# Attention, MLP, Fourier mixer and MLP on one core: steps of the query's tail, the mixers and the last pass in other slots, 32 adds on another engine

## The chip, the cores and the metric

The kernel runs on one core of a Trainium2 chip. What counts is the device time of one execution in microseconds, as the median of several runs. TensorE (PE in the profile) does the matmuls; VectorE (DVE), ScalarE (ACT) and GpSimd (POOL) work on tiles in SBUF, and the first two read the matmuls' results from PSUM banks; SyncE (SP) issues most of the DMAs in the order in which they are written.

## The reference

Three blocks stand one behind the other, each for 8 batches of 576 positions and 512 features:

```python
# 1. attention with 32 landmarks for each of 8 heads
A, Bm, C = sm(q, k_lm), sm(q_lm, k_lm), sm(q_lm, k)
Z = Bm.T / (norm1(Bm) * norminf(Bm) + 1e-6)
for _ in range(6):
    Z = 2 * Z - Z @ Bm @ Z
x = A @ Z @ C @ v
# 2. low-rank mix over positions, then an MLP of width 2048
u = x + (x.T @ U @ V).T
x = u + relu(u @ w_ch1) @ w_ch2
# 3. real part of a 2D Fourier transform, normalised, then a second MLP
u = x + real(fft(fft(x, axis=1), axis=2))
un = (u - mean(u)) / sqrt(var(u) + 1e-6)
out = u + relu(un @ w2_ch1) @ w2_ch2
```

The MLP weights come as 64-bit numbers.

## The kernel before

Every product of f32 matrices is made of three matmuls on high and low parts (`split`: ACT copies the high part, another engine subtracts it to get the low one). The 4608 positions are cut into 9 chunks of 512 columns, and an MLP pass (`Mlp.stream`) runs over the chunks with half of the hidden width: for each hidden block `up` does 12 matmuls (lines 299 to 301), ACT the relu (303) and DVE its low part (304); 4 output blocks follow (348 to 350) and DVE adds the residual (358). There are two such passes for the first MLP and one for the second; the second MLP's other half is done by `quarters`, a scheme with 7 products for two chunks in place of 8, in 10 units: chunk 0 alone, then four pairs, for p = 0 and again for p = 1. Each unit has slots of 6 matmuls, 16 in a unit of one chunk and 30 in one of two; `prepare` makes the next unit's high and low parts, `load` fetches chunks, and `down` adds the outputs: `get_res` loads an earlier partial result, `plant` has ACT copy it into a PSUM bank (538), `mul` adds three matmuls a block to it (547 to 549).

Everything is ordered by hand: nothing is moved by a scheduler. A stream gives way after each hidden or output block, that is after 12 matmuls: this is a slot. `Slots` is a table of (slot, step), and at each slot the steps of other work that are due are issued behind the stream's matmuls, on whichever engines they use. Every engine runs its own instructions in the order in which they were issued.

- The attention's `Batch.steps` (one batch every 16 slots, beside the first pass) has, at the end of each batch: normalising the query's scores A (`query_norm`, line 885 on DVE) at slot 12, transposing them (`query_t`, 891 and ACT's copies 893), their last 64 rows (`query_tail`, 900 and ACT's copies 903) at slot 14, and their products with U (`mixed`, 914) at slot 15. `query_tail` and `mixed` both use the bank "b", of which there is one. The Newton steps (932, 937) run beside them.
- `Mixer.steps` (one batch every 24 slots, from slot 33 of the second pass on) loads a batch of the first MLP's result (`load`, tile U), folds it by symmetry over features and positions (`fold_d` 1066, `fold_t` 1076), splits that (`fold_split`, tiles h and l with e or o for the even and odd part), makes a special row (`fold_row`), and multiplies by cosine and sine tables (`over_d`, matmuls 76 to 78, the row's at 1107). It ends with `unfold`, `store`, and the normalisation of two halves: `mean` (1160) sums over features with a matmul and DVE reads it (1170). `mean` uses the bank "l", of which there is one; the products use "f", of which there are two.
- `convert`, `single` and `stage` take weights from 64-bit integers to high and low f32 parts in five steps on DVE, ACT and POOL and put them to DRAM for the pass to come; `bufs` is the number of their buffers. Between them DVE waits for POOL's add (104 or 135).

On SP the loads for a chunk, the stores (213 to 216, 226), weight fetches (255, 88), the staged weights (119) and U's load (1057) stand in one queue, and a store waits at its head until its data is there.

Of the kernel before, what the change touches and what calls it, by code (L numbers as in the profile page):

```python
# [39 lines left out]
def body(ctx: ExitStack, tc: tile.TileContext, qT, kT, vn, mU, mV, w11, w12, w21, w22,  # L40
# [49 lines left out]
    def convert(cv, raw, out, bufs=1):  # L90
# [12 lines left out]
        nc.vector.scalar_tensor_tensor(out=pf, in0=lo, scalar=2.0 ** -52, in1=pf, op0=ALU.mult, op1=ALU.mult)  # L103
        nc.gpsimd.tensor_tensor(pf, pf, af, op=ALU.add)  # L104
        yield 1
# [15 lines left out]
    def single(cv, raw, out, bufs):  # L121
# [12 lines left out]
        nc.vector.scalar_tensor_tensor(out=pf, in0=lo, scalar=2.0 ** -52, in1=pf, op0=ALU.mult, op1=ALU.mult)  # L134
        nc.gpsimd.tensor_tensor(pf, pf, af, op=ALU.add)
        yield 1
# [99 lines left out]
    class Mlp:  # L236
# [154 lines left out]
        def quarters(self, tail, ys, w1s, w2s, dst):  # L391
# [89 lines left out]
            def up_two(i, s0, g):  # L481
# [23 lines left out]
                for q in range(2):  # L505
# [9 lines left out]
                    rectify(g, (0, 2 + q), B("e", q), s0 + 12 + q)  # L515

            def down(i, s0, g):
                p, unit = units[i]
                seed = i > 0
                res, skip, sc, ps, out = {}, {}, {}, {}, {}  # L520
                outs = [(h, d) for h in reversed(range(len(unit))) for d in range(4)]

                def get_res(j, c, d):
                    res[j] = lp.tile([P, NC], F32, name="res", bufs=4)
                    ys[p].get(c, d, res[j])

# [40 lines left out]
                for j, (h, d) in enumerate(outs):  # L567
                    c, s = unit[h], s0 + 2 * j
                    lag = 0 if end and j + 1 == len(outs) else 1
                    at(max(s - 10, s0 - 8 + j), lambda j=j, c=c, d=d: get_res(j, c, d))  # L570
                    at(s - 4, lambda j=j: plant(j))
# [23 lines left out]
            for i, (p, unit) in enumerate(units):  # L595
# [3 lines left out]
                def begin(i=i, s0=s0, g=g, two=two, last=last):  # L599
                    (up_two if two else up_one)(i, s0, g)  # L600
                    down(i, s0 + (14 if two else 8), g)
                    if i + 1 < len(units):
                        prepare(i + 1, s0, (2, 4, 13, 16, 19, 22, 25) if two else range(2, 16, 2) if i else range(7, 21, 2))
                    if i + 2 < len(units):
                        for key, s in (((0, 0), 10), ((1, 0), 24), ((1, 1), 27), ((0, 1), 29)):
                            if not two:
                                s = {10: 8, 24: 14, 27: 17, 29: 19}[s] + (5 if i == 0 else 0)
                            if key[0] < len(units[i + 2][1]):
                                at(s0 + s, lambda key=key: load(i + 2, key))
                    if last:  # L610
                        for n in range(7):
                            at(s0 + 2 * n + 3, lambda n=n: (self.w1.append(0), self.w1.pop(), self.fetch("w1", w1s[n])))
                        for d in range(4):
                            at(s0 + 24 + 2 * d, lambda d=d: self.fetch("w2", w2s[d]))
# [60 lines left out]
    class Batch:  # L675
# [308 lines left out]
        def steps(self, after):  # L984
# [8 lines left out]
            if not a:  # L993
# [6 lines left out]
                        (11, lambda: self.query_norm(H0)), (12, self.values), (12, lambda: self.query_norm(H1)),  # L1000
                        (13, lambda: self.query_t(0)), (14, lambda: self.query_t(1)), (14, self.query_tail),
                        (15, self.mixed), (16 - b, self.heads), (17 - b, self.rank))
# [41 lines left out]
    class Mixer:  # L1044
# [33 lines left out]
        def fold_split(self, nm):  # L1078
            h = self.fp.tile([P, 2, NF], F32R, name=f"h{nm}", bufs=1)
            l = self.fp.tile([P, 2, NF], F32R, name=f"l{nm}", bufs=1)  # L1080
            split(h, l, self.c[nm][:, :, 0:NF])
            self.lhs[nm] = (h, l)

        def fold_row(self):
            fp, U = self.fp, self.U
            row = fp.tile([1, NF], F32, name="top", bufs=1)
            nc.vector.tensor_tensor(row[:, 1:HS], U[0:1, 2, 1:HS], U[0:1, 2, S - 1:HS:-1], op=ALU.add)
            nc.scalar.copy(row[:, 0:NF:HS], U[0:1, 2, 0:NF:HS])
            both = self.f["row"]
            nc.scalar.copy(both[0:1], row)  # L1090
            low = fp.tile([1, NF], F32, name="rl", bufs=1)
            nc.vector.tensor_tensor(low, row, f32(both[0:1]), op=ALU.subtract)
            nc.scalar.copy(both[32:33], low)
# [64 lines left out]
        def mean(self, n):  # L1158
            ps = self.bank("l", 1)[:, 0:HS]
            nc.tensor.matmul(ps, self.f["ones"], self.half[n]["a"][:, 0, :], start=True, stop=True)  # L1160
            return ps
# [38 lines left out]
        def steps(self):  # L1200
            yield from ((0, self.load), (4, lambda: self.fold_d("e")), (4, lambda: self.fold_d("o")),
                        (5, lambda: self.fold_t("e")), (6, lambda: self.fold_split("e")), (6, self.fold_row),
                        (7, lambda: self.fold_t("o")), (8, lambda: self.fold_split("o")))
            yield from ((8 + 3 * (nm == "o") + i, lambda nm=nm, i=i: self.over_d(nm, i)) for nm in "eo"
                        for i in range(3))
            yield from ((14, self.top_row), (15, lambda: self.odd(0)), (16, lambda: self.even(0)),
# [245 lines left out]
```

## Time and profile before

| | |
|---|---|
| median of 3 runs | 1869.18 us (1866.18 to 1873.06) |
| profiled execution, its own time | 1866.1 us |
| its span in the trace | 1864.1 us |
| TensorE busy | 1824.5 us, 98% |
| DVE, ACT, POOL busy | 1024.1, 708.3, 376.2 us |

The span is the time from the first to the last instruction of the trace, 2.0 us less than the execution's own time. In the trace the attention ends at about 470 us, the mixers lie between 686 and 1322, and the quarters begin at 1485. A row of a timeline has the start, the length, the engine, the line of the kernel, the operation and its tiles (out<-in); in brackets stands how long the engine idled before it, and for whom. Instructions that belong together are drawn as one row with a count.

### The profile page before, as it was taken

The numbers are of one execution on the slowest core, as the hardware profiler recorded it, in microseconds if no ns is written. First come the engines' busy times: TensorE is split into PE (matmuls) and PEld (weight loads), VectorE is DVE, ScalarE is ACT, GpSimd is POOL, SyncE is SP. The second block draws the span as 40 slices with busy tenths as digits, with TensorE's granted clock in tenths as the row PEclk, the third lists the DMA queues.
The fourth block names the chain that finished last, engine by engine and source line by source line (L and its number), as shares of the span: only waits on it lengthen the run. The fifth ranks groups of instructions, "written<-read, shape, count | busy, mean of one in ns | idle before, by whom it ended". The sixth has DMA issues, their size and how long they took to land.

```text
span 1864.1 us, 30739 instructions
## 1 busy us (share of the span) xinstructions
PE 1824.5 (98%) x12152; PEld 1482.5 (80%) x12152; DVE 1024.1 (55%) x1764; ACT 708.3 (38%) x1469; POOL 376.2 (20%) x355
## 2 busy tenths in 40 slices
PE   6899999999999999999999999999999999999999
PEld 5777777777888887887887888888888888887887
DVE  7897565555323334755555464475432275438774
ACT  3544443444312212323333243333322266545542
POOL 3334211221201222323122142332311000000000
PEclk9999999999999999999999999999999999999999
DMA  7455445452537343434535553442432564477765
GB/s 266 140 179 162 148 168 201 143 172 98 172 124 276 125 135 113 153 111 168 170 128 190 220 176 137 142 150 79 167 111 88 183 193 157 144 259 226 225 198 158
DMA packets 175391, 305.56 MB, mean 164 GB/s; under 512 B 27440, under 2 KB 92560, under 8 KB 175248
## 3 DMA queue, kind: packets, MB, share of 16 engines
q1 hardware_dynamic: 170640, 294.17, 47.6%
q10 hardware_dynamic: 4608, 9.44, 1.3%
q8 instruction: 95, 1.56, 0.4%
q14 instruction: 48, 0.39, 0.1%
HBM read 195.74 MB, written 107.22 MB: 163 GB/s over the span
## 4 chain that ended last, share of the span: by engine, by line
PE 87%; DVE 5%; DMA 3%; ACT 3%; issue 1%; SPq 0%; POOL 0%; ACTq 0%; DVEq 0%
PE ps L348 10%; PE ps L349 10%; PE ps L350 10%; PE ps L299 9%; PE ps L301 9%; PE ps L300 9%; PE ps L549 3%; PE ps L547 3%; PE ps L548 3%; PE ps L387 3%; PE ps L389 3%; PE ps L388 3%; PE ps_f L76 1%; PE ps_f L77 1%; DMA U<-x 1%; PE ps_f L78 1%
## 5 line engine op out<-in xcount | busy, mean ns | idle before, releaser
L348 PE MATMUL ps<-g,w 128*128 128x512 f32 x864 | 345.5, 400 | 0.0
L299 PE MATMUL ps<-x,w 128*128 128x512 f32 x864 | 345.4, 400 | 0.0
L350 PE MATMUL ps<-g,w 128*128 128x512 f32 x864 | 338.5, 392 | 0.6 <-DVE g L304 0.6
L349 PE MATMUL ps<-g,w 128*128 128x512 f32 x864 | 338.1, 391 | 0.0
L301 PE MATMUL ps<-x,w 128*128 128x512 f32 x864 | 337.3, 390 | 0.0
L300 PE MATMUL ps<-x,w 128*128 128x512 f32 x864 | 337.0, 390 | 0.0
L304 DVE SCALAR_TENSOR_TENSOR g<-ps,g 128x512 fp32r<-128x512 f32 x216 | 148.7, 689 | 334.6 <-ACT g L303 333.9
L303 ACT ACTIVATE g<-ps 128x512 fp32r<-128x512 f32 x216 | 129.0, 597 | 368.2 <-PE ps L301 367.8
L348 PEld LDWEIGHTS ps<-g,w 128*128 128x128 f32 x864 | 162.9, 189 | 37.6 <-issue 3.5
L350 PEld LDWEIGHTS ps<-g,w 128*128 128x128 f32 x864 | 163.0, 189 | 36.3 <-DVE g L304 1.0
L301 PEld LDWEIGHTS ps<-x,w 128*128 128x128 f32 x864 | 162.2, 188 | 35.0
L299 PEld LDWEIGHTS ps<-x,w 128*128 128x128 f32 x864 | 162.2, 188 | 34.4
L349 PEld LDWEIGHTS ps<-g,w 128*128 128x128 f32 x864 | 163.2, 189 | 32.2
L300 PEld LDWEIGHTS ps<-x,w 128*128 128x128 f32 x864 | 162.5, 188 | 31.5
L104 POOL TENSOR_TENSOR cvp<-cvp,cva 128x512 f32<-128x512 f32 x56 | 72.8, 1300 | 380.8 <-DVE cvp L103 380.8
L358 DVE TENSOR_TENSOR xf<-ps,xf 128x512 f32<-128x512 f32 x76 | 52.4, 689 | 120.3 <-PE ps L350 116.8
L549 PE MATMUL ps<-g,w 128*128 128x512 f32 x288 | 112.3, 390 | 2.0 <-DVE g L457 2.0
L547 PE MATMUL ps<-g,w 128*128 128x512 f32 x288 | 112.3, 390 | 1.1 <-ACT ps L538 1.0
L52 POOL TENSOR_TENSOR x<-xf,x 128x512 fp32r<-128x512 f32 (+7 forms) x56 | 67.8, 1213 | 220.8 <-ACT x L51 193.8
L548 PE MATMUL ps<-g,w 128*128 128x512 f32 x288 | 112.0, 389 | 0.0
L52 POOL TENSOR_TENSOR stg<-cva,stg 128x512 fp32r<-128x512 f32 x40 | 57.3, 1433 | 68.4 <-ACT stg L51 66.7
L101 ACT ACTIVATE wraw<-wraw 128x512 f32<-128x512 f32 x48 | 32.7, 681 | 91.2 <-DVE cva L97 88.1
(325 smaller groups left out, 2915.9 us busy)
## 6 DMA issues: line engine op xcount, KB each, us to landing
d<-stg SPq DMA_DIRECT2D x54, 512.0 KB
w<-d SPq DMA_DIRECT2D x54, 512.0 KB
wraw<-w SPq DMA_DIRECT2D x48, 512.0 KB
y<-xf SPq DMA_DIRECT2D x76, 256.0 KB
res<-y SPq DMA_DIRECT2D x72, 256.0 KB
xf<-y SPq DMA_DIRECT2D x40, 256.0 KB
u<-u1T ACTq DMA_DIRECT2D x32, 288.0 KB
U<-x SPq DMA_DIRECT2D x8, 1152.0 KB
```

What stands on the lines that cost most here:

```text
L52: (eng or nc.vector).tensor_tensor(lo, src, f32(hi), op=ALU.subtract)
L299: nc.tensor.matmul(ps, wh, xh, start=k == 0, stop=False)
L300: nc.tensor.matmul(ps, wl, xh, start=False, stop=False)
L301: nc.tensor.matmul(ps, wh, xl, start=False, stop=k == 3)
L303: nc.scalar.activation(g[:, 0, :], ps, AF.Relu)
L304: nc.vector.scalar_tensor_tensor(out=g[:, 1, :], in0=ps, scalar=0.0, in1=f32(g[:, 0, :]), op0=ALU.max, op1=ALU.subtract)
L348: nc.tensor.matmul(ps, wh, gh, start=k == m0, stop=False)
L349: nc.tensor.matmul(ps, wl, gh, start=False, stop=False)
L350: nc.tensor.matmul(ps, wh, gl, start=False, stop=k == m1 - 1)
L547: nc.tensor.matmul(ps[j], wh, gh, start=first, stop=False, skip_group_check=True)
L548: nc.tensor.matmul(ps[j], wl, gh, start=False, stop=False, skip_group_check=True)
L549: nc.tensor.matmul(ps[j], wh, gl, start=False, stop=k == ks[3], skip_group_check=True)
```

## The change

It has four parts. In the attention `query_tail` is issued at slot 13 in place of 14. In the mixers U's load goes a slot earlier than the mixer's first (not for batch 0), the folds and the splits of their parts go a slot later and their high and low parts are steps of their own, the products follow from slot 9 instead of 8, and `mean` takes its bank from "f". In the conversions with one buffer the add goes from POOL to DVE. In the quarters, `res` of a unit of one chunk is loaded at the end of the unit before, and `prepare` and `load` have other slots at the unit bounds. The lines of the changed kernel are numbered 15 higher behind `quarters` and 23 higher behind `fold_row`.

```diff
@@ -101,7 +101,7 @@
         nc.scalar.activation(f32(hi), f32(hi), AF.Abs)
         pf, af = f32(p), f32(a)
         nc.vector.scalar_tensor_tensor(out=pf, in0=lo, scalar=2.0 ** -52, in1=pf, op0=ALU.mult, op1=ALU.mult)
-        nc.gpsimd.tensor_tensor(pf, pf, af, op=ALU.add)
+        (nc.gpsimd if bufs > 1 else nc.vector).tensor_tensor(pf, pf, af, op=ALU.add)
         yield 1
         nc.vector.scalar_tensor_tensor(out=af, in0=f32(hi), scalar=MINNORM, in1=pf, op0=ALU.is_ge, op1=ALU.mult)
         yield 1
@@ -132,7 +132,7 @@
         nc.scalar.activation(f32(hi), f32(hi), AF.Abs)
         pf, af = f32(p), f32(a)
         nc.vector.scalar_tensor_tensor(out=pf, in0=lo, scalar=2.0 ** -52, in1=pf, op0=ALU.mult, op1=ALU.mult)
-        nc.gpsimd.tensor_tensor(pf, pf, af, op=ALU.add)
+        nc.vector.tensor_tensor(pf, pf, af, op=ALU.add)
         yield 1
         nc.vector.scalar_tensor_tensor(out=out, in0=f32(hi), scalar=MINNORM, in1=pf, op0=ALU.is_ge, op1=ALU.mult)
         yield 1
@@ -514,15 +514,22 @@
                         rectify(g, key, T, s)
                     rectify(g, (0, 2 + q), B("e", q), s0 + 12 + q)
 
+            former = {}
+
+            def order(unit):
+                return [(h, d) for h in reversed(range(len(unit))) for d in range(4)]
+
+            def get_res(i, j):
+                p, unit = units[i]
+                h, d = order(unit)[j]
+                t = former.setdefault(i, {})[j] = lp.tile([P, NC], F32, name="res", bufs=4)
+                ys[p].get(unit[h], d, t)
+
             def down(i, s0, g):
                 p, unit = units[i]
                 seed = i > 0
-                res, skip, sc, ps, out = {}, {}, {}, {}, {}
-                outs = [(h, d) for h in reversed(range(len(unit))) for d in range(4)]
-
-                def get_res(j, c, d):
-                    res[j] = lp.tile([P, NC], F32, name="res", bufs=4)
-                    ys[p].get(c, d, res[j])
+                skip, sc, ps, out = {}, {}, {}, {}
+                outs, res = order(unit), former.setdefault(i, {})
 
                 def get_skip(j, c, d):
                     skip[j] = lp.tile([P, NC], F32, name="skip", bufs=4)
@@ -567,7 +574,8 @@
                 for j, (h, d) in enumerate(outs):
                     c, s = unit[h], s0 + 2 * j
                     lag = 0 if end and j + 1 == len(outs) else 1
-                    at(max(s - 10, s0 - 8 + j), lambda j=j, c=c, d=d: get_res(j, c, d))
+                    if len(unit) == 2 or i == 0:
+                        at(max(s - 10, s0 - 8 + j), lambda j=j: get_res(i, j))
                     at(s - 4, lambda j=j: plant(j))
                     for half in range(2):
                         at(s + half, lambda j=j, h=h, d=d, half=half: mul(j, h, d, half))
@@ -598,13 +606,20 @@
 
                 def begin(i=i, s0=s0, g=g, two=two, last=last):
                     (up_two if two else up_one)(i, s0, g)
+                    if i + 1 < len(units) and len(units[i + 1][1]) == 1:
+                        for j in range(4):
+                            at(s0 + 25 + j, lambda j=j: get_res(i + 1, j))
                     down(i, s0 + (14 if two else 8), g)
                     if i + 1 < len(units):
-                        prepare(i + 1, s0, (2, 4, 13, 16, 19, 22, 25) if two else range(2, 16, 2) if i else range(7, 21, 2))
+                        if two:
+                            starts = (2, 4, 13, 16, 19, 22, 25) if len(units[i - 1][1]) == 2 else (5, 13, 15, 17, 19, 22, 25)
+                        else:
+                            starts = (2, 4, 9, 11, 13, 15, 17) if i else range(8, 22, 2)
+                        prepare(i + 1, s0, starts)
                     if i + 2 < len(units):
                         for key, s in (((0, 0), 10), ((1, 0), 24), ((1, 1), 27), ((0, 1), 29)):
                             if not two:
-                                s = {10: 8, 24: 14, 27: 17, 29: 19}[s] + (5 if i == 0 else 0)
+                                s = {10: 8, 24: 18, 27: 20, 29: 22}[s] + (5 if i == 0 else 0)
                             if key[0] < len(units[i + 2][1]):
                                 at(s0 + s, lambda key=key: load(i + 2, key))
                     if last:
@@ -998,7 +1013,7 @@
                         (9, lambda: self.query_exp(H0)), (9, self.scores_sum), (10, lambda: self.scores_t(0)), (10, lambda: self.query(2)),
                         (11, lambda: self.scores_t(1)), (11, self.scores_tail), (11, lambda: self.query_exp(H1)),
                         (11, lambda: self.query_norm(H0)), (12, self.values), (12, lambda: self.query_norm(H1)),
-                        (13, lambda: self.query_t(0)), (14, lambda: self.query_t(1)), (14, self.query_tail),
+                        (13, lambda: self.query_t(0)), (13, self.query_tail), (14, lambda: self.query_t(1)),
                         (15, self.mixed), (16 - b, self.heads), (17 - b, self.rank))
             if self.b:
                 yield 13, lambda: self.mlp.get_tail(self.b)
@@ -1078,18 +1093,26 @@
         def fold_split(self, nm):
             h = self.fp.tile([P, 2, NF], F32R, name=f"h{nm}", bufs=1)
             l = self.fp.tile([P, 2, NF], F32R, name=f"l{nm}", bufs=1)
-            split(h, l, self.c[nm][:, :, 0:NF])
+            nc.scalar.copy(h, self.c[nm][:, :, 0:NF])
             self.lhs[nm] = (h, l)
 
+        def fold_low(self, nm):
+            h, l = self.lhs[nm]
+            nc.vector.tensor_tensor(l, self.c[nm][:, :, 0:NF], f32(h), op=ALU.subtract)
+
         def fold_row(self):
-            fp, U = self.fp, self.U
-            row = fp.tile([1, NF], F32, name="top", bufs=1)
+            U = self.U
+            self.row = row = self.fp.tile([1, NF], F32, name="top", bufs=1)
             nc.vector.tensor_tensor(row[:, 1:HS], U[0:1, 2, 1:HS], U[0:1, 2, S - 1:HS:-1], op=ALU.add)
             nc.scalar.copy(row[:, 0:NF:HS], U[0:1, 2, 0:NF:HS])
+
+        def row_high(self):
+            nc.scalar.copy(self.f["row"][0:1], self.row)
+
+        def row_low(self):
             both = self.f["row"]
-            nc.scalar.copy(both[0:1], row)
-            low = fp.tile([1, NF], F32, name="rl", bufs=1)
-            nc.vector.tensor_tensor(low, row, f32(both[0:1]), op=ALU.subtract)
+            low = self.fp.tile([1, NF], F32, name="rl", bufs=1)
+            nc.vector.tensor_tensor(low, self.row, f32(both[0:1]), op=ALU.subtract)
             nc.scalar.copy(both[32:33], low)
 
         def over_d(self, nm, i):
@@ -1156,7 +1179,7 @@
             nc.vector.tensor_tensor(a[:, 0, :], a[:, 0, :], a[:, 1, :], op=ALU.add)
 
         def mean(self, n):
-            ps = self.bank("l", 1)[:, 0:HS]
+            ps = self.bank("l")[:, 0:HS]
             nc.tensor.matmul(ps, self.f["ones"], self.half[n]["a"][:, 0, :], start=True, stop=True)
             return ps
 
@@ -1198,11 +1221,12 @@
             nc.sync.dma_start(rs[self.b][:, self.cols(n)], self.half[n]["r"])
 
         def steps(self):
-            yield from ((0, self.load), (4, lambda: self.fold_d("e")), (4, lambda: self.fold_d("o")),
-                        (5, lambda: self.fold_t("e")), (6, lambda: self.fold_split("e")), (6, self.fold_row),
-                        (7, lambda: self.fold_t("o")), (8, lambda: self.fold_split("o")))
-            yield from ((8 + 3 * (nm == "o") + i, lambda nm=nm, i=i: self.over_d(nm, i)) for nm in "eo"
-                        for i in range(3))
+            yield from ((-1 if self.b else 0, self.load), (5, lambda: self.fold_d("e")), (5, lambda: self.fold_d("o")),
+                        (6, lambda: self.fold_t("e")), (6, self.fold_row), (7, lambda: self.fold_split("e")),
+                        (7, self.row_high), (8, lambda: self.fold_low("e")), (8, self.row_low),
+                        (7, lambda: self.fold_t("o")), (8, lambda: self.fold_split("o")), (9, lambda: self.fold_low("o")))
+            yield from ((s, lambda nm=nm, i=i: self.over_d(nm, i)) for s, nm, i in
+                        ((9, "e", 0), (10, "e", 1), (11, "e", 2), (12, "o", 0), (13, "o", 1), (13, "o", 2)))
             yield from ((14, self.top_row), (15, lambda: self.odd(0)), (16, lambda: self.even(0)),
                         (17, lambda: self.unfold(0)), (17, lambda: self.unfold(2)), (17, lambda: self.odd(1)),
                         (18, lambda: self.even(1)), (19, lambda: self.unfold(1)), (19, lambda: self.unfold(3)),
```

On TensorE, in a batch of the attention: x and w belong to the MLP's stream, ps_n to a Newton step, ps_c to `query_t`, ps_b to `query_tail`. Before:

```order
L301 MATMUL ps<-x,w_256 128x512
L932 MATMUL ps_n<-ry 32x64 x8
L891 MATMUL ps_c<-ident_sb,A 128x128 x4
L299 MATMUL ps<-x,w_257 128x512
L300 MATMUL ps<-x,w_257 128x512
...
L301 MATMUL ps<-x,w_257 128x512
L932 MATMUL ps_n<-ry 32x32 x8
L891 MATMUL ps_c<-ident_sb,A 128x128 x4
L900 MATMUL ps_b<-ident_sb,A 64x64 x4
L348 MATMUL ps<-g,w_258 128x512
```

And of the changed kernel:

```order
L301 MATMUL ps<-x,w_256 128x512
L947 MATMUL ps_n<-ry 32x64 x8
L906 MATMUL ps_c<-ident_sb,A 128x128 x4
L915 MATMUL ps_b<-ident_sb,A 64x64 x4
L299 MATMUL ps<-x,w_257 128x512
...
L300 MATMUL ps<-x,w_257 128x512
L301 MATMUL ps<-x,w_257 128x512
L947 MATMUL ps_n<-ry 32x32 x8
L906 MATMUL ps_c<-ident_sb,A 128x128 x4
L348 MATMUL ps<-g,w_258 128x512
```

The tail's four matmuls moved from behind the second transposition to behind the first, ahead of a block of 12 matmuls of the stream.

On DVE, at the fold of mixer 0: L304 is the MLP's, L358 its residual add, x and xf its next chunk, wraw, cva and cvp a weight that is converted, big and cc the folds, le, lo and rl the low parts. Before:

```order
L304 SCALAR_TENSOR_TENSOR g<-ps,g 128x512
L1066 TENSOR_TENSOR big<-U 128x1152
L106 SCALAR_TENSOR_TENSOR cva<-wraw,cvp 128x512
L304 SCALAR_TENSOR_TENSOR g<-ps,g 128x512
L1076 TENSOR_TENSOR cc<-big 128x2x287
L304 SCALAR_TENSOR_TENSOR g<-ps,g 128x512
L52 TENSOR_TENSOR le<-cc,he 128x578
L1087 TENSOR_TENSOR top<-U 1x287
L1092 TENSOR_TENSOR rl<-top,row 1x289
L52 TENSOR_TENSOR x<-xf,x 128x512
L358 TENSOR_TENSOR xf<-ps,xf 128x512
L52 TENSOR_TENSOR lo<-cc,ho 128x578
```

And of the changed kernel:

```order
L104 TENSOR_TENSOR cvp<-cvp,cva 128x512
L304 SCALAR_TENSOR_TENSOR g<-ps,g 128x512
L106 SCALAR_TENSOR_TENSOR cva<-wraw,cvp 128x512
L304 SCALAR_TENSOR_TENSOR g<-ps,g 128x512
L1081 TENSOR_TENSOR big<-U 128x1152
L304 SCALAR_TENSOR_TENSOR g<-ps,g 128x512
L1091 TENSOR_TENSOR cc<-big 128x2x287
L1106 TENSOR_TENSOR top<-U 1x287
L52 TENSOR_TENSOR x<-xf,x 128x512
L358 TENSOR_TENSOR xf<-ps,xf 128x512
L1101 TENSOR_TENSOR le<-cc,he 128x578
L1115 TENSOR_TENSOR rl<-top,row 1x289
```

The fold of U stands one L304 lower, the low parts `le` and `rl` stand behind the split of x and the residual add instead of ahead of them, and the conversion's add (L104) has come onto this queue.

On SP, around the end of mixer 1 and the load of U for mixer 2: x_3 and x_4 are results of the first MLP, u_1 the mixed batch, d_9 a staged weight, un_184 its normalised half. Before:

```order
L1146 DMA u_1_176<-U 128x4x576
...
L216 DMA x_4_74<-xf 1x256
L119 DMA d_9_146<-stg 128x1024
L88 DMA wraw<-w 128x1024
L223 DMA xf<-y_5_83 128x512 x4
L1195 DMA un_184<-Z 128x4x288
L1057 DMA U<-x_2_72 128x4x576
L1195 DMA un_184<-Z 128x4x288
```

And of the changed kernel:

```order
L1169 DMA u_1_176<-U 128x4x576
...
L216 DMA x_4_74<-xf 1x256
L1072 DMA U<-x_2_72 128x4x576
L119 DMA d_9_146<-stg 128x1024
L88 DMA wraw<-w 128x1024
L223 DMA xf<-y_5_83 128x512 x4
L1218 DMA un_184<-Z 128x4x288 x2
```

The load of U moved from between the stores of the two halves to right behind the last store of x_4, ahead of the staging's two DMAs and the stream's loads.

## Rows read from the trace of the kernel before

**Rows 1.** The page, part 1: busy time, share and count by engine.

```profile
PE 1824.5 (98%) x12152; PEld 1482.5 (80%) x12152; DVE 1024.1 (55%) x1764; ACT 708.3 (38%) x1469; POOL 376.2 (20%) x355
```

**Rows 2.** Waits of PE: releaser; total us, times, longest.

```profile
PE ps_b L914 <- ACT at L903: 4.1, 7, 1.8
PE ps_f L1107 <- ACT row L1093: 3.0, 3, 1.0
...
PE ps_l L1160 <- DVE Z L1170: 2.2, 2, 1.1
PE ps L549 <- DVE g L457: 2.0, 2, 1.7
...
PE ps_f L77 <- DVE le L52: 1.4, 3, 0.5
PE ps L547 <- ACT ps L538: 1.0, 1, 1.0
PE ps L350 <- DVE g L304: 0.6, 1, 0.6
```

**Rows 3.** PE timeline, mixer 0: start, us, line, [idle before <-releaser].

```profile
698.55 0.40 PE L348 MATMUL ps<-g,w 128*128 128x512 f32 x1
698.78 0.40 PE L349 MATMUL ps<-g,w 128*128 128x512 f32 x1
699.74 0.49 PE L350 MATMUL ps<-g,w 128*128 128x512 f32 x1 [0.56 <-DVE g L304]
...
702.72 0.43 PE L1107 MATMUL ps_f<-tabh,row 128*97 128x258 f32 x1 [0.99 <-ACT row L1093]
```

**Rows 4.** Windows: length, busy us (instructions) by engine, PEclk, DMA share, GB/s.

```profile
86.00:96.00 10.00, 8.11 (x136) 6.42 (x132) 8.96 (x15) 6.45 (x18) 7.00 (x10) 0.83 0.01 2
696.00:706.00 10.00, 7.91 (x30) 5.74 (x30) 6.80 (x9) 4.51 (x10) 6.72 (x6) 0.84 0.34 114
1676.00:1690.00 14.00, 10.88 (x44) 7.83 (x44) 9.19 (x15) 7.87 (x15) 0.00 (x0) 1.00 0.80 279
```

**Rows 5.** Timeline of batch 1.

```profile
80.78 0.48 PE L299 MATMUL ps<-x,w 128*128 128x512 f32 x1
...
81.62 0.82 DVE L885 TENSOR_TENSOR A<-A,sr 128x640 f32<-128x640 f32 x1
...
85.60 0.43 PE L932 MATMUL ps_n<-ry 32*32 32x64 f32 x16 [1.80 <-DVE ry L937]
```

**Rows 6.** Timeline of batch 2.

```profile
139.56 0.82 DVE L885 TENSOR_TENSOR A<-A,sr 128x640 f32<-128x640 f32 x1
...
139.72 0.48 PE L299 MATMUL ps<-x,w 128*128 128x512 f32 x1
```

**Rows 7.** Timeline of batch 5.

```profile
322.03 0.82 DVE L885 TENSOR_TENSOR A<-A,sr 128x640 f32<-128x640 f32 x1
...
322.56 0.48 PE L299 MATMUL ps<-x,w 128*128 128x512 f32 x1
```

**Rows 8.** DVE and POOL in the timeline, mixer 0.

```profile
693.97 1.36 DVE L1066 TENSOR_TENSOR big<-U 128x1152 f32<-128x1152 f32 x1 [2.48 <-DMA U<-x]
...
694.01 2.60 POOL L1066 TENSOR_TENSOR big<-U 128x576 f32<-128x576 f32 x1 [1.82 <-DMA U<-x]
...
695.25 1.92 DVE L106 SCALAR_TENSOR_TENSOR cva<-wraw,cvp 128x512 f32<-128x512 f32 x1
```

**Rows 9.** SP's timeline, around the load of U for mixer 2.

```profile
835.56 5.43 SPq L216 DMA_DIRECT2D x<-xf  x1
...
846.89 0.44 SPq L1057 DMA_DIRECT2D U<-x  x1
```

**Rows 10.** The page, part 5: busy us, mean ns.

```profile
L104 POOL TENSOR_TENSOR cvp<-cvp,cva 128x512 f32<-128x512 f32 x56 | 72.8, 1300 | 380.8 <-DVE cvp L103 380.8
...
L358 DVE TENSOR_TENSOR xf<-ps,xf 128x512 f32<-128x512 f32 x76 | 52.4, 689 | 120.3 <-PE ps L350 116.8
```

**Rows 11.** ACT timeline, quarters, unit 5.

```profile
1681.53 0.59 ACT L538 COPY ps<-res 128x512 f32<-128x512 f32 x1 [4.63 <-DMA res<-y]
```

## The prediction

> **What bounds the kernel now.** I read the busy shares first: TensorE is busy in 1824.5 of 1864.1 us, 98%, and no other engine is above 55% but its own weight loads [rows 1]. So the time is the matmuls plus what TensorE idles, 39.6 us, and a change that leaves the matmuls alone can win only there or in the clock. Next the waits of TensorE, by what it waited for [rows 2]. The diff touches seven of these rows: L914, L1107, L1160, L549, L77, L547 and L350, 4.1 + 3.0 + 2.2 + 2.0 + 1.4 + 1.0 + 0.6 = 14.3 us in 7 + 3 + 2 + 2 + 3 + 1 + 1 = 19 waits. Such a row understates the loss: two matmuls in a row start 0.23 us apart though each is drawn 0.40 us long [rows 3], so an idle of x costs x + 0.17. With 19 × 0.17 = 3.2 the 19 waits cost 17.5 us. By stage: attention (L914) 4.1 + 7 × 0.17 = 5.3; mixers 7.2 + 9 × 0.17 = 8.7; quarters 3.0 + 3 × 0.17 = 3.5.
>
> Last I looked at the granted clock in windows around those places [rows 4]. After the waits of batch 1 it averages 0.83 over 10 us, after those of mixer 0 0.84, so 10 × 0.17 = 1.7 and 10 × 0.16 = 1.6 us are lost to a spell at 1.2 in place of 2.4 GHz. In the quarters 14 us with 3 us of idle stay at 1.00. So a wait does not always cost clock, and I treat the clock as a term apart.
>
> **The change, part by part. Tail of the query.** `mixed` (L914) waits for ACT's copies (L903) of the one bank "b" that `query_tail` has just filled; with the tail a slot sooner those four copies have a slot more, 12 matmuls × 0.23 = 2.8 us, and the longest of the seven waits was 1.8. All seven should go: −5.3. The tail's four small matmuls now stand where the first `L299` stood, and they need A as normalised by DVE's L885. TensorE stops for that, with everything behind it on its queue, if L885 is late. Batch 1: L885 ends at 82.44, TensorE is there at 80.78, 1.66 late, but 5 us on TensorE waits 1.80 for a Newton step that DVE sets [rows 5], so this is idle moved, not added. Batch 2: 140.38 against 139.72, 0.66 late [rows 6]. Batch 5: 322.85 against 322.56, 0.29 late [rows 7]. In batches 3, 4, 6 and 7 the same pair of rows has L885 done first, and batch 0 idles there at start-up anyhow. Together +1.0; bounds 0 and 1.66 + 6 × 0.66 = 5.6.
>
> **Mixers.** DVE's fold of mixer 0 waits 2.48 us for U and holds the MLP's `L304` that is behind it [rows 8]; that is the wait of L350. U's load goes a slot or more earlier, ahead of the staging DMAs on SP: for mixer 2 SP comes free of the waiting L216 at 841.0 and issues U only at 846.89 [rows 9], now right behind it, some 5 us sooner. What SP is moved past are one staging write, one weight fetch and four loads for the stream, put off by one issue of 0.44 us. The fold itself begins a slot later (4 to 5). Mixer 0: without the wait it could begin at 693.97 − 2.48 + 2.76 = 694.25, 0.28 later than now, while its first product (slot 8 to 9) comes 2.76 later. Of this gain of 2.48, an x split and a residual add that now stand ahead of `le` on DVE take 2 × 0.69 = 1.4 (the price of such an operation is in [rows 10]), which leaves about 1.1 against the 0.5 that L77 waited at most; `rl` stands right behind `le` on DVE, and the row's copies on ACT then have the three products of a slot less to wait for. I take the waits of L77, L350 and L1107 as gone. The mean moves from one bank to two, so that a matmul no longer waits for DVE to read the other half's mean (L1160). Together −8.7. The margins are under 1 us, and DVE's rows before are no guide to mixers 1, 3, 5 and 7, which showed no such wait. I take eight new waits of 0.1, +0.8; bounds 0 and 8 × 0.99 = 7.9, the longest that a mixer shows [rows 3].
>
> **Adds from POOL to DVE.** In the conversions with one buffer 24 adds at L104 and 8 at L135 move. On POOL one takes 1300 ns, and a DVE operation of two inputs on the same tile 689 [rows 10]: POOL −41.6 us, DVE +22 us, 55% to 57% of the span. All lie from the mixers on, where DVE is busy 6.80 of 10 us [rows 4]; the staged weights are used a pass later, so nothing but DVE's queue carries the cost to TensorE. What hides it is DVE's 3.2 us in 10. If the cover is gone at an add, its 0.69 lies in front of an L304 that a matmul waits for. Taken at 0; bounds −0.6 and +22, the former because DVE's L106 no longer waits there for POOL, so that an L304 behind it could save a wait like that of L350.
>
> **Quarters.** Unit 5 is the first with p = 1. Its first `res` came to ACT 4.63 us late [rows 11], behind it stood the relu, and the three waits of TensorE in [rows 2] at L547 and L549 are this place. The loads move to the end of unit 4, 5 to 6 slots of 6 × 0.23 = 1.4 us sooner, 7 us where 4.63 were missing. −3.5. The preparation at the other unit bounds is spread out, and a few loads come up to 4 slots later; in unit 0 one is issued in the slot of its first use. One new wait of the size of L547's, +1.0; bounds 0 and 3.5.
>
> **Clock.** The spell after mixer 0 goes with all three waits before it: −1.6. That of batch 1 has lost one of its two waits; half of it, −0.85. Together −2.4; bounds 0 and −3.3.
>
> The Trainium skill, *SBUF — State Buffer*, section *SBUF: two separate sides*, speaks against the moved adds: DVE and GpSimd share one port pair as an exclusive lock, and a DVE operation with two SBUF inputs is held for the whole of a GpSimd operation that reads SBUF. The trace agrees where they met: the L106 at 695.25 took 1.92 us [rows 8] with the fold on POOL beside it from 694.01 on, against 0.69 for a two-input operation by itself [rows 10]. By this rule an add that meets such a fold costs the 1.92; were it so for all 32, the time would be that of rival 4.
>
> **The sum**, against the profiled execution's own 1866.1: −17.5 − 2.4 + 1.0 + 0.8 + 1.0 = −17.1, so 1849.0. The median of the three runs, 1869.18, is 3.1 above that execution; **1852**.
>
> **The rivals.** (1) *The tail's wait takes the place of `mixed`'s.* L885 late by 0.66 in six batches and 1.66 in batch 1 without being repaid: 5.6 for the 1.0 counted, and the spell of batch 1 stays, +0.85: 1852 + 4.6 + 0.85 = 1857. For it [rows 5 to 7]; against it the 1.80 at 85.60, and the four batches where A is early.
> (2) *The mixers' waits come back a slot later.* The low parts have moved behind other work on DVE, and 7.9 of the 8.7 return, with the clock's 1.6: 1852 + 7.9 − 0.8 + 1.6 = 1861. For it: margins under 1 us; against: U no longer late.
> (3) *The removed waits did not set the end.* TensorE then waits as long elsewhere and nothing changes: 1869. Against it the 98%.
> (4) *Slower: DVE's queue becomes the bound in the mixers*, through the 32 adds. If x of each reaches TensorE, the gain of 17.1 is used up at x = 17.1 / 32 = 0.53 us, and the kernel is slower by 0.5% from (17.1 + 9.3) / 32 = 0.83. With 0.69 each it ends at 1852 + 22 = 1874; held to 1.92 each, 1852 + 61 = 1913. For it: L304 feeds the matmuls from this queue; against: the 3.2 idle us of 10. The lock that the Trainium skill states, *SBUF — State Buffer*, section *SBUF: two separate sides*, is what would raise the price to the second figure.
>
> **How the numbers follow.** A measurement of this kernel can tell about 0.5%, 9.3 us, from no change: faster is below 1859.8, slower above 1878.5. Forecast 0.60 (1846 to 1857), rival 1 0.14, rival 2 0.12, rival 3 0.10, rival 4 0.04. Faster: 0.60, 0.11 of rival 1 and 0.03 of rival 2, 0.74. Slower: 0.03 of rival 4. Same: the rest, 0.23. The range begins at 1847, where the bounds of the gains meet (17.5 + 3.3 off the own time, 1.0 on, is 1846) and the runs' own spread leaves a little; it ends at 1862, beyond rival 2, and leaves out rival 3 and most of rival 4.
>
> **What would show it.** Right: no row of TensorE's waits for L914, L1107, L1160, L77 or L547; DVE's fold without a wait for U; a clock of 1.00 after mixer 0; DVE about 1046 us busy, POOL about 335; a span near 1847. Tail wrong: waits of the tail's matmuls (line 915) for A. Mixers wrong: waits at the products for `le` or `row`, one slot later. Adds wrong: waits of TensorE for L304 or for x in the stretches with conversions. Quarters wrong: waits for `xf` or `res` at unit bounds. What would make me wrong most: margins of some tenths in the odd mixers, which no row of before shows.

## The result and the profile after

The changed kernel takes 1850.56 us (median of 6 runs, 1849.01 to 1851.76), the kernel before 1866.58 (6 runs, 1864.63 to 1873.06). The ratio is 0.9907, 95% interval 0.9892 to 0.9923: 16.0 us less. The profiled execution of the changed kernel took 1851.76 us, its span is 1849.9.

The busy shares (the page's first part) answer to [rows 1]:

```profile
PE 1819.8 (98%) x12152; PEld 1481.9 (80%) x12152; DVE 1041.0 (56%) x1796; ACT 706.6 (38%) x1469; POOL 327.8 (18%) x323
```

The matmuls are the same 12152. DVE has the 32 new instructions and 16.9 us more, POOL 48.4 us less. TensorE's waits, which answer to [rows 2], as line, releaser, total us, times, longest:

```profile
PE ps_b L738 <- POOL qb L722: 11.4, 2, 10.0
PE ps_b L915 <- DVE A L900: 3.6, 4, 1.7
PE ps_n L771 <- ACT u1T L992: 2.9, 1, 2.9
PE ps_c L875 <- issue: 2.4, 1, 2.4
PE ps_n L771 <- ACT x L51: 2.1, 1, 2.1
PE ps_n L973 <- DVE W L964: 1.5, 1, 1.5
PE ps_n L947 <- DVE ry L952: 1.1, 3, 0.6
PE ps_f L1130 <- ACT row L1116: 0.4, 1, 0.4
```

The seven rows that the prediction named are gone but for one 0.4 at the mixers' row; nothing of the quarters is left. L738, L875 and the 2.9 at L771 belong to the start-up and stood before too (the last with 1.8). New are the tail's own wait (L915 for A) and, at the end of batch 1, L973 (the products with W) and the 2.1 at L771 (the norms of batch 2). How long DVE's fold sat idle for U (total us, times), in the kernel before

```profile
  DMA U<-x: 9.5, 3
```

and in the changed kernel:

```profile
  DMA U<-x: 0.7, 1
```

The three were 2.48, 2.27 and 4.74 us in mixers 0, 2 and 4, those with waits of TensorE; the one that is left is mixer 0's, whose load is not moved. The windows that answer to [rows 4]: us, busy us by engine, clock.

```profile
86.00:96.00 10.00, 9.62 (x175) 7.75 (x173) 9.90 (x18) 5.96 (x14) 6.16 (x9) 1.00 0.09 28
106.00:116.00 10.00, 7.92 (x66) 4.34 (x65) 9.76 (x20) 4.49 (x10) 2.81 (x2) 0.83 0.65 224
690.00:706.00 16.00, 16.00 (x76) 13.28 (x75) 13.32 (x17) 7.80 (x17) 10.93 (x7) 1.00 0.52 172
1670.00:1690.00 20.00, 20.00 (x90) 16.57 (x89) 16.87 (x28) 10.62 (x20) 0.00 (x0) 1.00 0.63 221
```

In mixer 0 and at unit 5 TensorE is busy without a pause and at full clock. In batch 1 the stretch from 86 is full now, but 20 us later there are 2.1 us idle and a spell of half clock (0.83) that was not there before.

Since both kernels have the same matmuls in the stream and the quarters, their starts can be laid beside each other. This table is worked out from the starts in the two traces, its last column before rounding:

| stretch | before, us | after, us | change |
|---|---|---|---|
| start to the stream's first matmul | 65.8 | 67.2 | +1.4 |
| to its 173rd (batch 1) | 71.3 | 72.2 | +0.9 |
| to its 1210th (batches 2 to 7) | 327.6 | 325.5 | −2.1 |
| to the first of the quarters (mixers) | 1020.6 | 1010.4 | −10.2 |
| to the last of the quarters | 373.9 | 369.7 | −4.3 |

Of the first row nothing can be laid to the change, of which it holds only batch 0's tail: over the 14 executions profiled here it lies between 65.8 and 69.2, and with the tail undone it is 67.1. So what a part of the change does is read below from a stretch between two matmuls, beside the time of the whole.

### The profile page after: what moved, and what is told of

Read it like the earlier page. It is cut to its first block, busy times and chain, and to the rows that moved or that the text cites. A ratio compares the mean times of both kernels' runs of the same rounds, so it can differ in the third digit from the quotient of the medians.

```text
span 1849.9 us, 30721 instructions
## 1 busy us (share of the span) xinstructions
PE 1819.8 (98%) x12152; PEld 1481.9 (80%) x12152; DVE 1041.0 (56%) x1796; ACT 706.6 (38%) x1469; POOL 327.8 (18%) x323
## 3 DMA queue, kind: packets, MB, share of 16 engines
q8 instruction: 95, 1.56, 0.3%
## 4 chain that ended last, share of the span: by engine, by line
PE 94%; DVE 4%; issue 1%; ACT 1%; DMA 0%; SPq 0%; POOL 0%; DVEq 0%; ACTq 0%
PE ps L299 11%; PE ps L348 11%; PE ps L350 10%; PE ps L349 10%; PE ps L300 10%; PE ps L301 10%; PE ps L554 4%; PE ps L556 4%; PE ps L555 4%; PE ps L387 3%; PE ps L389 3%; PE ps L388 3%; PE ps_f L76 1%; PE ps_f L77 1%; PE ps_f L78 1%; PE ps_c L875 1%
## 5 line engine op out<-in xcount | busy, mean ns | idle before, releaser
L304 DVE SCALAR_TENSOR_TENSOR g<-ps,g 128x512 fp32r<-128x512 f32 x216 | 148.9, 690 | 348.5 <-ACT g L303 348.1
L358 DVE TENSOR_TENSOR xf<-ps,xf 128x512 f32<-128x512 f32 x76 | 52.4, 689 | 112.4 <-PE ps L350 110.4
L104 POOL TENSOR_TENSOR cvp<-cvp,cva 128x512 f32<-128x512 f32 x32 | 41.7, 1303 | 166.8 <-DVE cvp L103 166.8
```

Of the source, the lines that this page charges most:

```text
L304: nc.vector.scalar_tensor_tensor(out=g[:, 1, :], in0=ps, scalar=0.0, in1=f32(g[:, 0, :]), op0=ALU.max, op1=ALU.subtract)
```

## The experiments

**The tail undone.**

```diff
-... (13, self.query_tail), (14, lambda: self.query_t(1)), ...
+... (14, lambda: self.query_t(1)), (14, self.query_tail), ...
```

> The changed kernel with query_tail back at slot 14. Theory: the tail's move gives little (DVE is 95% busy in batches 1 and 2 and only passes its lateness to another wait); against the changed kernel's 1850.6 this run is 0 to 2 us slower, near 1851.5; the seven waits at mixed come back with some 4.1 us, those of the tail (3.6 us) go, and of batch 1 the sum of TensorE's waits stays within 1 us. Rival: the move was worth its 5.3 less 1.0, hidden by start-up differences; then 1855.

Measured: 1852.61 (5 runs), ratio to before 0.9923 (0.991 to 0.9937), 2.0 above the changed kernel, inside the two intervals. TensorE's waits:

```profile
PE ps_n L947 <- DVE ry L952: 5.1, 4, 2.7
PE ps_b L929 <- ACT at L918: 3.9, 7, 1.7
...
PE ps_n L771 <- DVE dg L764: 1.7, 1, 1.7
```

The seven waits are back with 3.9. The wait at the norms (L771) is there too, with 1.7: it does not come from the tail's move. Batch 1 takes 71.36 us against 71.2 to 71.3 in the kernels with the tail moved and the clock full: no gain there. Batches 2 to 7 take 328.2 against 325.5: 2.8 gained there. The theory holds for batch 1 and was low for the others. Two traces with the tail at slot 14 differ by 0.7 in batches 2 to 7 (327.6 in the kernel before), so the gain there is 2.1 to 2.8.

**The mixers undone**: the whole class of before put back into the changed kernel (the diff is the mixers' part of the change, reversed).

> The changed kernel with the whole Mixer class of before (load, folds, bank of the mean). Theory: its waits are the mixers' gain, so the 9 waits of before come back (7.2 us drawn, 8.7 with their starts) and the low clock after mixer 0: 1850.6 + 10.2 = 1861. Rival: DVE's adds taken off POOL had part in it, so that the folds on POOL are no longer in DVE's way and less comes back: 1855 to 1857.

Measured: 1860.68 (5 runs), ratio 0.9968 (0.9956 to 0.9981), 10.1 above the changed kernel. Its waits between 680 and 1322 us:

```profile
PE ps_f L1122 <- ACT row L1108: 3.0, 3, 1.0
PE ps_l L1175 <- DVE Z L1185: 2.1, 2, 1.0
PE ps_f L77 <- DVE le L52: 1.5, 3, 0.5
PE ps L350 <- DVE g L304: 0.9, 2, 0.6
```

The same waits as in [rows 2], with the adds on DVE, so the adds had no part in removing them. From the 1210th matmul to the last it takes 1389.1 against 1380.1 in the changed kernel, 9.0 more (1379.7 to 1380.9 in the other kernels here with the same mixers and quarters). The half-clock spell after mixer 0 did not come back: the waits were the same and the clock stayed at 1.00.

**The quarters undone**, in the same way.

> The changed kernel with the quarters of before. Theory: the four waits at unit 5 come back, 3.1 us drawn and 4.3 between the same matmuls of the two traces: 1850.6 + 4.3 = 1854.9. Rival: another load or prepare step hides them here, since all comes 10 us sooner: 1851.

Measured: 1856.39 (5 runs), ratio 0.9945 (0.9932 to 0.9957), 5.8 above the changed kernel. Between the two profiled executions 2.0 us lie ahead of the stream's first matmul. In the quarters:

```profile
PE ps L549 <- DVE g L457: 2.0, 2, 1.7
```

Between the same matmuls 3.05 us come back at unit 5 and nothing anywhere else. So the waits belong to these loads; the one at L547 did not return here.

**The adds back on POOL.**

```diff
-(nc.gpsimd if bufs > 1 else nc.vector).tensor_tensor(pf, pf, af, op=ALU.add)
+nc.gpsimd.tensor_tensor(pf, pf, af, op=ALU.add)
...
-nc.vector.tensor_tensor(pf, pf, af, op=ALU.add)
+nc.gpsimd.tensor_tensor(pf, pf, af, op=ALU.add)
```

> The changed kernel with the 32 adds back on POOL. Theory: they lie beside TensorE's work on either engine, so the time stays at 1850.6 within 1 us and no new wait of TensorE above 0.5 us shows. Rival: the adds on POOL held DVE in the folds, and a wait for le, row or L304 at an even mixer returns with 1 to 3 us: 1852 to 1854.

Measured: 1850.47 (4 runs), ratio 0.9915 (0.9902 to 0.9929): no difference to the changed kernel. Its trace has a wait of 0.8 for `le` in mixer 5 and 0.6 for the row in mixer 2, 1.1 us more from the 1210th matmul on. That is more than the theory allowed and may be the rival's effect, but another kernel here with the adds on DVE (the one with less work in batch 2's sums, below) has 0.8 more there by a wait of its own, so 1.1 is hardly clear of what traces differ by. The groups of the moved adds and of the fold, in the changed kernel (count, ns least/median/most, first and last start):

```profile
L104 DVE TENSOR_TENSOR cvp<-cvp,cva x24: 691/692/694, 602.6 to 1412.6; 128x512 f32<-128x512 f32 x24
...
L135 DVE TENSOR_TENSOR cvp<-cvp,cva x8: 692/693/694, 1056.0 to 1327.2; 128x512 f32<-128x512 f32 x8
...
L1081 DVE TENSOR_TENSOR big<-U x8: 1346/1352/2622, 694.2 to 1241.2; 128x1152 f32<-128x1152 f32 x8
```

and the fold with the adds on POOL:

```profile
L1081 DVE TENSOR_TENSOR big<-U x8: 1348/1724/2583, 691.9 to 1238.8; 128x1152 f32<-128x1152 f32 x8
```

None of the 32 adds on DVE was ever held: only two overlap an operation of POOL, and both had begun first. With the adds on POOL DVE's folds meet POOL's more often, 1724 ns for 1352 in the median, 1.9 us in all eight. The larger difference is at the select behind the add (L106, which waits for it), here in the changed kernel and then with the adds on POOL:

```profile
L106 DVE SCALAR_TENSOR_TENSOR cva<-wraw,cvp x48: 677/684/1641, 106.8 to 1413.8; 128x512 f32<-128x512 f32 x48
```

```profile
L106 DVE SCALAR_TENSOR_TENSOR cva<-wraw,cvp x48: 678/692/1999, 105.4 to 1413.0; 128x512 f32<-128x512 f32 x48
```

Added up, these 48 selects take 5.7 us less in the changed kernel: three of them no longer stand beside a fold on POOL that makes them 1.9 us long. Other operations became longer by less, so DVE gained only 17 us of work for 32 × 0.692 = 22.1.

**Three parts of the mixers by themselves.** U's load back at slot 0:

```diff
-... (-1 if self.b else 0, self.load), ...
+... (0, self.load), ...
```

> The changed kernel with U's load back at slot 0 of each mixer; all else as changed. Theory: the fold a slot later already gives U most of the time it lacked; U would land at about 850 for a fold due at 852 in mixer 2 and at 1008 to 1009.5 for one due at 1007.5 in mixer 4, so one wait of 0 to 1.5 us: 1850.6 to 1852. Rival: the earlier load is what removes the waits; then those of mixers 2 and 4 come back, 0.5 + 1.0 and 0.3 + 1.0 with 4 x 0.17: 1854.

One buffer for the mean:

```diff
-ps = self.bank("l")[:, 0:HS]
+ps = self.bank("l", 1)[:, 0:HS]
```

> The changed kernel with one buffer for the mean's bank. Theory: the two waits at the mean come back, 2.2 us drawn and 2.6 with their starts, at the same two halves: 1853. Rival: with U and the folds elsewhere DVE reads the mean in time: 1850.6.

The folds of before, with U sooner and two buffers for the mean:

```diff
-... (-1 if self.b else 0, self.load), (5, fold_d ...), ... (9, "e", 0) ...
+... (-1 if self.b else 0, self.load), (4, fold_d ...), ... (8, "e", 0) ...
```

> The changed kernel with the folds, splits and products of before (fold at slot 4, products from 8), but U loaded sooner and two buffers for the mean. Theory: the waits for le and row come from U's lateness, which is left in mixer 0 alone (its load is not moved): 0.6 + 0.5 + 1.0 and 3 x 0.17 = 2.6, with the low clock behind them 4.2: 1853 to 1855, and no wait in mixers 2 and 4. Rival: the order of the folds is what makes them; then all seven waits come back, 5.0 + 7 x 0.17 + 1.6 = 7.8: 1858.

Measured: 1853.15, 1853.02 and 1852.82 us (4 runs each), ratios 0.9927 (0.9909 to 0.9944), 0.9926 (0.9911 to 0.9941), 0.9923 (0.9905 to 0.9941): the times can't tell them apart, the traces can. TensorE's waits between 680 and 1322 us, first with the load at slot 0:

```profile
PE ps_f L1130 <- ACT row L1116: 0.3, 1, 0.3
```

then with one buffer:

```profile
PE ps_l L1183 <- DVE Z L1193: 2.1, 2, 1.0
PE ps_f L1130 <- ACT row L1116: 0.4, 1, 0.4
```

and with the folds of before:

```profile
PE ps_f L1122 <- ACT row L1108: 1.3, 2, 1.0
PE ps L350 <- DVE g L304: 0.5, 1, 0.5
PE ps_f L77 <- DVE le L52: 0.5, 1, 0.5
```

From the 1210th matmul to the last they take 1379.9, 1382.5 and 1382.8 us, against 1380.1 in the changed kernel: 0, 2.4 and 2.8. With the folds of before only mixer 0, whose load is not moved, has its three waits again (0.3 in mixer 2). So by the traces each of the three theories held, but for the low clock behind mixer 0, which stayed away; the median with the load at slot 0 lay 1.2 above its range. The three parts add up to 5.2 of the mixers' 9.0. The other 3.8 are about the waits of mixers 2 and 4 (five waits, each with its late start: 0.46 + 0.71 + 1.15 + 0.58 + 1.16 = 4.06 in the trace with the mixers undone): either the sooner load or the later fold removes them, so undoing one alone shows next to nothing.

**The select behind each moved add, four times** (for the fourth rival's price):

```diff
-nc.vector.scalar_tensor_tensor(out=af, in0=f32(hi), scalar=MINNORM, in1=pf, ...)
+for _ in range(4 if bufs == 1 else 1):
+    nc.vector.scalar_tensor_tensor(out=af, in0=f32(hi), scalar=MINNORM, in1=pf, ...)
```

and the same at the other eight.

> The changed kernel in which each of the 32 conversions with one buffer does its select on DVE (the operation behind the moved add) four times, with the same result: 96 more DVE operations of 0.69 us, +66 us of DVE, three times what the change moved there. Theory: DVE's idle time covers most of it, since a matmul waits only where such an operation lies ahead of a fold's low part or an L304 that is due: 0 to 10 us, 1851 to 1861. Rival (the fourth of the prediction): it reaches TensorE in full, 1850.6 + 66 = 1917.

Measured: 1861.82 (8 runs), ratio 0.9975 (0.9965 to 0.9985), 11.3 above the changed kernel, 10.3 of it by the traces from the 1210th matmul on. Busy shares, and waits between 680 and 1330 us:

```profile
PE 1822.2 (98%) x12152; PEld 1480.6 (80%) x12152; DVE 1105.1 (59%) x1892; ACT 704.9 (38%) x1469; POOL 330.3 (18%) x323
...
PE ps_f L77 <- DVE le L1103: 3.8, 3, 1.9
PE ps_l L1185 <- DVE cc L1181: 2.7, 2, 1.3
PE ps_f L1132 <- ACT row L1118: 1.2, 2, 0.6
```

64 us more of DVE cost 11.3, a sixth, by the waits nearly all at the folds' low parts, the row and the mean. The cover that the prediction named exists, and its end is at these three places.

**What bounds batch 1.** Less work for DVE in batch 2's landmark sums, which fall into batch 1's stretch:

```diff
+src = src.rearrange("p e (m w) -> p e m w", w=W)
-nc.vector.tensor_reduce(s_, src.rearrange("p e (m w) -> p e m w", w=W), axis=AX.X, op=ALU.add)
+nc.vector.tensor_reduce(s_, src[:, :, :, 0:2] if self.b == 2 else src, axis=AX.X, op=ALU.add)
```

> The changed kernel in which batch 2's four landmark sums on DVE run over 2 of 18 positions of each landmark (so batch 2 isn't the reference's): about 4 x 1.15 = 4.6 us less on DVE between 83 and 96 us. Read between the first matmul of the stream and its 173rd, which took 71.2 to 71.4 us with the full clock in the changed kernel and in those with one part undone, and 72.2 to 72.4 with a spell of half clock there. Theory: in batch 1 DVE sets the time, so the tail's move could only pass the wait on; then with less for DVE the stretch is 2.5 to 4.6 us shorter, 66.7 to 69. Rival: the order of the steps on TensorE and ACT's copies set it: 70.5 to 71.5.

Measured: 1847.32 (one run), and the stretch takes 67.5 us. The window from 66 to 140 us of the changed kernel, in which DVE is busy 69.0 of 74 us:

```profile
66.00:140.00 74.00, 68.53 (x933) 51.96 (x934) 69.03 (x134) 37.10 (x91) 29.00 (x28) 0.98 0.51 176
```

and with less for DVE:

```profile
66.00:140.00 74.00, 71.67 (x972) 54.79 (x971) 68.41 (x144) 40.55 (x98) 28.97 (x28) 1.00 0.51 175
```

The four sums took 0.27 us each in place of 1.34, so 4.3 us came off DVE and not the 4.6 that were expected; 3.7 of them reach the end, and TensorE is busy 3.1 us more in the same 74. DVE sets this stretch. Not all of its busy time is work. In the changed kernel two low parts of equal size follow each other, of which the first takes 0.61 us and the second, which begins beside POOL's split, 1.71:

```profile
108.00 2.24 DVE L52 TENSOR_TENSOR x<-u1T,x 128x448 fp32r<-128x448 f32 x2
...
108.22 1.54 POOL L52 TENSOR_TENSOR w<-cva,w 128x512 fp32r<-128x512 f32 x1 [2.55 <-ACT w L51]
```

**Two ways to relieve it.** Two of batch 1's low parts of x (the hand-over from the attention to the MLP) on POOL, and batch 2's norms a slot later:

```diff
-... nc.gpsimd if k % 2 and c > 1 else nc.vector)
+... nc.gpsimd if k % 2 else nc.vector)
```

> The changed kernel with two of batch 1's four low parts of the hand-over (128x448, 1.1 us each on DVE) on POOL, as it is for the later batches. Theory of a full DVE: the wait at the norms (2.0 us, behind two of these) falls by 1.1 and the same stretch by 1 to 2 us, to 69.5 to 70.3 at full clock, and the time to 1849. Rival: POOL is late with them and TensorE waits for x instead: no change or 1 us longer.

```diff
-yield 6, self.norms
+yield 6 + (self.b == 2), self.norms
```

> The changed kernel with batch 2's norms on TensorE a slot later (7 in place of 6). Theory of a full DVE: the wait of 2.0 us at the norms goes but its time comes back at the scores or the residue, the stretch stays within 0.7 us of 71.3. Rival: it is a matter of order alone, and the stretch is 2 us shorter, 69.3, and the time 1848.5.

The first edit does more than its text says: two of batch 0's low parts go to POOL as well, one of them at the start of the stretch.

Measured: 1849.17 and 1850.26 us (4 runs each), ratios 0.9907 (0.989 to 0.9925) and 0.9907 (0.9892 to 0.9921); stretches of 70.6 and 70.9 us against 71.3. The first got 0.6 where 1 to 2 were expected, the second 0.4: its wait at the norms went, and 0.6, 0.5 and 0.3 came at the scores, an `x` and a Newton step.

**Both, and two copies from DVE to ACT:**

```diff
-nc.vector.tensor_copy(self.au, ...
+(nc.scalar.copy if self.b == 1 else nc.vector.tensor_copy)(self.au, ...
```

and the same for W (both are copies of small products from PSUM), with the two edits above.

> The changed kernel with the last two edits together (two low parts of batch 1 on POOL, batch 2's norms a slot later) and batch 1's copies of au and W on ACT instead of DVE: 2 x 1.0 + 0.21 + 0.41 = 2.6 us less on DVE in batch 1. Theory of a full DVE: the waits at W (1.4) and at the norms go, and the stretch between the stream's first and 173rd matmul is 2 to 2.6 us shorter than 71.3, 68.7 to 69.3; the time 1848 to 1849. Rival: the two edits' gains of 0.6 and 0.4 don't add up and the waits pass on: 70.3 to 71, and 1850.

Measured: 1850.38 (5 runs), ratio 0.9912 (0.9897 to 0.9927), no better than the changed kernel; the stretch takes 70.4, 0.9 less than 71.3. The rival's range was right: the two edits' 0.6 and 0.4 nearly add up, and the two copies brought nothing more. DVE is busy 70.0 us between 66 and 140, against 69.0 in the changed kernel, although work was taken off it. Its timeline:

```profile
106.33 1.16 POOL L52 TENSOR_TENSOR x<-u1T,x 128x448 fp32r<-128x448 f32 x1 [0.39 <-ACT x L51]
106.47 1.58 DVE L97 SCALAR_TENSOR_TENSOR cva<-wraw,cva 128x512 uint32<-128x512 uint32 x1
...
107.97 0.68 DVE L106 SCALAR_TENSOR_TENSOR cva<-wraw,cvp 128x512 f32<-128x512 f32 x1
...
108.68 0.62 ACT L51 CAST w<-cva 128x512 fp32r<-128x512 f32 x1 [2.42 <-DVE cva L106]
...
109.77 0.68 ACT L992 COPY u1T<-ps_n 128x288 f32<-128x288 f32 x2
110.34 0.71 ACT L992 COPY u1T<-ps_c 128x288 f32<-128x288 f32 x2
110.80 0.46 PEld L802 LDWEIGHTS ps_c<-k__918,qb 64*32 64x32 f32 x16 [2.64 <-ACT u1T L992]
110.80 1.36 PE L802 MATMUL ps_c<-k__918,qb 64*32 64x512 f32 x16 [2.13 <-ACT u1T L992]
```

The part that went to POOL starts at 106.33, and DVE's L97 beside it takes 1.58 us, against 0.69 in the changed kernel:

```profile
106.19 0.69 DVE L97 SCALAR_TENSOR_TENSOR cva<-wraw,cva 128x512 uint32<-128x512 uint32 x1
```

L106 behind it is late, so ACT's cast waits 2.42, so its copies of u1T are late, and the scores, which need the bank that these copies read, wait 2.13. This agrees with the lock between DVE and GpSimd that the Trainium skill states (*SBUF — State Buffer*, section *SBUF: two separate sides*): the L97 begins behind POOL's operation and ends 0.56 us after it. It was met by relieving DVE, not by loading it. That this one hold is why the whole gained nothing is argued from the order of the rows; no run takes it away by itself.

## Why the prediction was right, and where it was not

**The whole.** 1852 was forecast, 1850.56 measured. Part of the nearness is chance. The 3.1 us added for the median of three runs shrank to 0.5 with six (1866.58 against 1866.1), and against the sum's own 1849.0 the profiled execution took 1851.76, with 1.4 of that before the stream begins and a spell of half clock in batch 1. And the errors of the terms partly cancel: between the two traces the attention (batches 1 to 7) gave 1.2 where the tail's terms and half a spell made 5.15, while the mixers gave 10.2 for 9.5 and the quarters 4.3 for 2.5.

**Tail.** Forecast −5.3 + 1.0 and half a spell; measured −2.8 against the kernel with the tail undone and −2.1 between the traces of before and after, all in batches 2 to 7. There the steps were right: 5.3 less batch 1's 1.9, plus 1.0, is −2.4, and the new waits were 0.2 and 0.2 where 0.66 and 0.29 were forecast (the first is 0.2 to 0.7 over the traces with the tail moved). The step that failed is in batch 1, where the 5.3 counts the wait at `mixed` with 1.9. The prediction calls the tail's wait there "idle moved, not added", and that was true (1.56, while the 1.80 at the Newton step fell to 0.4); but the same holds of the wait removed at `mixed`. With DVE full, its 1.75 turned up as 1.44 at W and 0.35 more at the norms (2.04 against 1.69 with the tail undone, in traces without a spell there). Rival 1 had the sum of batch 1 right, but by another way: the tail's wait was repaid, and it was the other one that was not saved.

**Mixers.** Forecast −8.7 + 0.8 − 1.6 = −9.5; measured −10.2 between the same matmuls of before and after, −10.1 by the times with the part undone and −9.0 by that run's trace, which has no spell. Eight new waits of 0.1 were one of 0.4. The grounds need two amendments. The wait at the row and `le` in mixers 2 and 4 hung on U's lateness, and the sooner load or the later fold removes it all but alone; in mixer 0, whose load stays, it is the later fold. The low clock after mixer 0 is not bound to its waits, since the same waits went without it twice. The mean's 2.6 was 2.4. The text ahead of the prediction says that `mean` takes its bank from "f"; it stays in "l", which has two buffers now.

**Adds.** Forecast 0 with DVE at +22 and POOL at −41.6; measured +0.1 by the times and −1.1 in the trace, DVE +17 and POOL −48.4, 7 of it at POOL's own folds. Not all adds lie from the mixers on, as the prediction says: four start between 602 and 665, ahead of the first mixer. The rival's break-even of 0.53 us for each of 32 operations was far off: 96 more operations cost 11.3, that is 0.12 for each. Had every add met a fold on POOL as the L106 at 695.25 did, it would have cost 1.92; no add was above 0.694.

**Quarters.** Forecast −3.5 + 1.0; measured −4.3 between the traces, −3.05 against the part undone, with no new wait. The mis-sized term is the +1.0. The −3.5 is low by 0.8 too, since an idle of x cost more than x + 0.17 here: behind the waits the next matmuls start 0.33 to 0.61 us apart in place of 0.23.

**Clock.** Forecast −2.4. The spell after mixer 0 went, and it had cost 1.6 (the kernel before against the one with the mixers undone, which has the same waits and no spell). That of batch 1, from which 0.85 was to be won, cost nothing that can be seen: the stretch took 71.27 with it in the kernel before and 71.36 with the tail undone and no spell, as fits a stretch that DVE sets. Another spell, 20 us later, came in 5 of the 8 profiled executions that had the tail moved and all of batch 1 as in the changed kernel, with 72.2 to 72.4 us in place of 71.3, a cost of 1.0. The two traces with the tail at slot 14 do not have it; they are too few to say whether the change brings it.

## What to carry to other kernels

A wait of the bounding engine was worth its length only where the engine waited for had slack, and in batch 1 it had none. So look at that engine's busy share in the window first, since a full one handed the wait on to its next consumer. Where two edits each cure the same wait, undoing one shows nothing; undo both, and read the trace between equal matmuls when the times can't tell. Work put on an engine with slack cost only what landed ahead of its few urgent instructions, here a sixth.

## What the runs showed that was not expected

DVE and POOL disturb each other in both directions of a move: taking adds off POOL shortened DVE's selects by 5.7 us in all and its folds by 1.9, and putting an operation on POOL made a DVE instruction of 0.69 us take 1.58. And the half-clock spells came or stayed away with the same instructions and the same waits before them, so their cost can't be read off the waits of one trace.
